# Running nearly all matmuls of an attention and feed-forward kernel as two 64-row array tiles

## Chip, core, metric

The kernel runs on one core of a Trainium2 chip. The metric is the device time of one execution in microseconds (us).

## The reference, cut to what matters

```python
# q: 8 x 16 x 384 x 64, k and v: 8 x 4 x 384 x 64 (each k/v head serves 4 q heads), float32
scores = (1/8) * q @ k.T
attn   = exp(scores - max) / sum
x      = attn @ v                    # then reordered to 3072 tokens x 1024
out    = relu(x @ w_in)**2 @ w_out   # w_in 1024 x 2048, w_out 2048 x 1024
```

There are 8 batches. The kernel works on head pairs, 8 to a batch, so 64 pairs in all. It leaves out the maximum, which the small inputs allow.

## The kernel before

A small recorder takes every operation with the buffers that it reads and writes, and puts in the semaphores. The order in which the program *adds* operations is the order in which each engine is given them. An instruction that waits holds up those behind it.

Scores of one pair are 64-row matmuls (a head has 64 dimensions), one head on the lower and one on the upper half of the array. They fill one stretch of 4.5 PSUM banks, and a single exponential empties it:

```python
def scores_pair(p):
    def piece(pe, x, j, c0, c1):                 # x: head of the pair, so array half
        rows = slice(64 * x, 64 * x + 64)
        return pe.matmul(sc_flat[:, x*half + j*S + c0 : ...], kt[rows, ...], qt[rows, c0:c1])
    first = run([(0, 2, 256, 384)], sc_keys)
    run([(1,1,0,384), (0,0,0,384), (1,2,0,128), (0,1,0,128), (1,2,128,384), (0,1,128,384)], sc_keys)
    run([(1,0,0,384), (0,2,0,256)], sc_keys, after=[first])
    R.add("scalar", lambda e: e.activation(dst, src, AF.Exp, scale=0.125), ...)   # 128 x 2304
```

All else contracts over 128 rows and uses the whole array: attention times V (`attend`, 18 matmuls of 65 columns a pair, into the accumulator bank `po`), the up projection (8 matmuls of 384 columns per output tile, then relu on VectorE and square on ScalarE) and the down projection (16 of 512 columns, then a copy on VectorE).

The main loop puts feed-forward work of the batch before between the pieces of each pair. `PER_PAIR` says how many ns of it. The second batch (`n // NPB == 1`) gets 2600 ns a pair, the later ones 4700 and 5100, because it must save some of the first batch's feed-forward for a pause (`LULL`) before the third batch, while q and k of that batch are transposed:

```python
PER_PAIR = {1: 2600.0, 2: 4700.0, **{b: 5100.0 for b in range(3, B + 1)}}
for n in range(NPB, NP + 1):                     # pair n; the first batch has code of its own
    if n == 2 * NPB:
        ...; prepare(2); prepare_v(2); fill(LULL)
    scores_pair(n)
    fill(per * 0.4);  attend(n - 1, 0)
    fill(per * 0.2);  attend(n - 1, 1);  put_x(n - 1)
    ...
    fill(per * 0.4)
while next(ffn, None): pass                      # the feed-forward of the last batch
```

The softmax here doesn't subtract the row's maximum and nothing guards it: scores larger than these inputs give would overflow.

## Time and profile before

| | before |
|---|---|
| median | 437.3 us |
| PE busy | 99% |
| ScalarE, VectorE busy | 46%, 37% |
| pair in the second batch | 3.87 us |
| pair in later batches | about 6.4 us |

The head of the page: busy us of each engine, share of the span and number of instructions; then the chain that ended last.

```profile
PE 429.8 (99%) x3637; PEld 239.9 (55%) x3637; DVE 160.7 (37%) x345; ACT 198.9 (46%) x210; POOL 48.2 (11%) x62
...
PE 97%; DVE 1%; DMA 1%; issue 0%; ACT 0%
```

TensorE is the limit. The groups of instructions say what it does (line, engine, operation, output and inputs, shapes, count | busy us, mean ns | idle us before them):

```profile
L433 PE MATMUL f_ps<-xT,w_in_sb 128*128 128x384 bf16 x1016 | 181.8, 326 | 1.0 <-DMA xT<-o_sb 1.0
...
L391 ACT ACTIVATE expT<-sc_ps 128x2304 bf16<-128x2304 f32 x56 | 116.8, 2085 | 105.1 <-PE sc_ps L374 103.3
...
L402 PE MATMUL po<-v_aug,expT 128*128 128x65 bf16 x1143 | 56.6, 194 | 0.7 <-DVE o_sb L415 0.4
```

A matmul's recorded 326 ns, whose end is modelled by the profiler, overlaps with the next. What it costs is the distance from one start to the next: 162 ns for 384 columns, 216 for 512, 32 for 65. The second batch's stretch of the chain (start us, us, what) is TensorE alone, with a pair every 3.87 us, although a pair's exponential takes 2.1 us of it:

```profile
43.44 0.60 PE sc_ps L374 x8
44.03 0.76 PE f_ps L433 x4
44.79 0.28 PE po L402 x9
45.07 0.65 PE f_ps L433 x4
45.72 0.28 PE po L402 x9
46.01 1.30 PE f_ps L433 x8
47.31 0.59 PE sc_ps L374 x8
```

The list of PE's waits (engine, what it writes and line <- what it waited for: us in total, times, longest) has none of scores for the exponential. Its only wait for `po`, 0.4 us, falls in the first batch:

```profile
PE f_ps L273 <- DVE warm L221: 1.1, 1, 1.1
PE f_ps L433 <- DMA xT<-o_sb: 1.0, 1, 1.0
PE po L402 <- DVE o_sb L415: 0.4, 1, 0.4
...
```

The scores are where TensorE loses time without waiting for anyone. In the timeline of a later batch (start, us, engine, line, operation, shapes, count):

```profile
202.83 0.65 PE L433 MATMUL f_ps<-xT,w_in_sb 128*128 128x384 bf16 x3
203.42 0.66 PE L374 MATMUL sc_ps<-qT,kT 64*128 64x128 bf16 x9
204.01 1.31 PE L433 MATMUL f_ps<-xT,w_in_sb 128*128 128x384 bf16 x7
```

The third up matmul starts at 203.158 by the trace. Its columns need until 203.32, but the scores start only at 203.416, 96 ns later; their last columns have run at 203.917, and the next whole-array matmul starts at 204.012, 95 ns later.

### The profile page before, as it was taken

The numbers are of one execution on the slowest core, as the hardware profiler recorded it, in microseconds if no ns is written. First come the engines' busy times: TensorE is split into PE (matmuls) and PEld (weight loads), VectorE is DVE, ScalarE is ACT, GpSimd is POOL, SyncE is SP. The second block draws the span as 40 slices with busy tenths as digits, with TensorE's granted clock in tenths as the row PEclk, the third lists the DMA queues.
The fourth block names the chain that finished last, engine by engine and source line by source line (L and its number), as shares of the span: only waits on it lengthen the run. The fifth ranks groups of instructions, "written<-read, shape, count | busy, mean of one in ns | idle before, by whom it ended". The sixth has DMA issues, their size and how long they took to land.

```text
span 435.2 us, 8284 instructions
## 1 busy us (share of the span) xinstructions
PE 429.8 (99%) x3637; PEld 239.9 (55%) x3637; DVE 160.7 (37%) x345; ACT 198.9 (46%) x210; POOL 48.2 (11%) x62
## 2 busy tenths in 40 slices
PE   8999999999999999999999999999999999999997
PEld 4666654565545654566555665456645565546544
DVE  2665423344223433244322442234422344224412
ACT  4866760466333663266423654335742565303400
POOL 5850001031000300022000300003000000000000
PEclk9999999999999999999999999999999999999999
DMA  8999999539721937229622756229462100120012
GB/s 228 196 197 204 188 182 197 149 34 105 175 85 50 118 71 125 85 54 114 128 83 69 98 72 144 69 89 115 47 153 68 59 20 20 58 91 24 2 56 88
DMA packets 96084, 44.71 MB, mean 103 GB/s; under 512 B 74416, under 2 KB 90032, under 8 KB 96048
## 3 DMA queue, kind: packets, MB, share of 16 engines
q0 software_dynamic: 34288, 16.65, 30.3%
q1 hardware_dynamic: 58720, 25.28, 25.0%
q10 hardware_dynamic: 3040, 2.26, 1.7%
q8 instruction: 28, 0.46, 0.5%
q14 instruction: 8, 0.07, 0.0%
HBM read 35.65 MB, written 12.58 MB: 111 GB/s over the span
## 4 chain that ended last, share of the span: by engine, by line
PE 97%; DVE 1%; DMA 1%; issue 0%; ACT 0%
PE f_ps L451 39%; PE f_ps L433 39%; PE po L402 8%; PE sc_ps L374 8%; PE f_ps L273 1%; PE sc_ps L357 1%; PE sc_ps L295 1%; DMA xT<-o_sb 1%; PE f_ps L295 0%; DVE o_sb L415 0%; PE sc_ps L433 0%; DVE qT L303 0%; ACT expT L363 0%; DVE kT L303 0%; DVE k_dup L320 0%
## 5 line engine op out<-in xcount | busy, mean ns | idle before, releaser
L433 PE MATMUL f_ps<-xT,w_in_sb 128*128 128x384 bf16 x1016 | 181.8, 326 | 1.0 <-DMA xT<-o_sb 1.0
L451 PE MATMUL f_ps<-w_out_sb,h2T 128*128 128x512 bf16 (+2 forms) x784 | 180.0, 375 | 0.0
L391 ACT ACTIVATE expT<-sc_ps 128x2304 bf16<-128x2304 f32 x56 | 116.8, 2085 | 105.1 <-PE sc_ps L374 103.3
L433 PEld LDWEIGHTS f_ps<-xT,w_in_sb 128*128 128x128 bf16 x1016 | 92.4, 98 | 61.6 <-issue 6.6
L442 ACT ACTIVATE h2T<-hr 128x384 bf16<-128x384 f32 x128 | 66.6, 521 | 101.1 <-DVE hr L440 99.5
L451 PEld LDWEIGHTS f_ps<-w_out_sb,h2T 128*128 128x128 bf16 x784 | 70.2, 97 | 75.9 <-issue 5.3
L440 DVE TENSOR_SCALAR hr<-f_ps 128x384 f32<-128x384 f32 x127 | 70.6, 557 | 105.8 <-PE f_ps L433 105.7
L459 DVE COPY y_sb<-f_ps 128x512 f32<-128x512 f32 (+2 forms) x49 | 33.4, 681 | 111.9 <-PE f_ps L451 111.4
L402 PEld LDWEIGHTS po<-v_aug,expT 128*128 128x128 bf16 x1143 | 51.8, 98 | 22.6 <-ACT expT L363 2.0
L402 PE MATMUL po<-v_aug,expT 128*128 128x65 bf16 x1143 | 56.6, 194 | 0.7 <-DVE o_sb L415 0.4
L374 PE MATMUL sc_ps<-qT,kT 64*128 64x128 bf16 (+2 forms) x504 | 37.2, 271 | 0.0
L415 DVE TENSOR_TENSOR o_sb<-po,rinv 128x384 bf16<-128x384 f32 x64 | 35.5, 554 | 2.2
L374 PEld LDWEIGHTS sc_ps<-qT,kT 64*128 64x128 bf16 x504 | 20.6, 94 | 21.4 <-issue 15.0
L412 DVE RECIPROCAL rinv<-po 128x6 f32<-128x6 f32 x64 | 12.2, 191 | 39.6 <-PE po L402 39.6
L167 POOL DMA_DIRECT2D k_st<-in_k_dram x7 | 5.4, 775 | 166.7 <-DMA xT<-o_sb 166.7
L363 ACT ACTIVATE expT<-sc_ps 128x768 bf16<-128x768 f32 x24 | 18.5, 810 | 3.1 <-PE sc_ps L357 2.5
L320 POOL COPY k_dup<-k_st 128x1536 bf16<-128x1536 bf16 x6 | 8.8, 1469 | 42.9 <-DMA k_st<-in_k_dram 42.9
L341 POOL COPY v_aug<-v_st 128x768 bf16<-128x768 bf16 x6 | 5.0, 832 | 43.0 <-DMA v_st<-in_v_dram 43.0
L357 PE MATMUL sc_ps<-qT,kT 64*128 64x384 bf16 x48 | 8.3, 341 | 0.2
L181 POOL DMA_DIRECT2D q_st<-in_q_dram x7 | 8.2, 1178 | 0.0
L273 PE MATMUL f_ps<-warm 128*128 128x256 bf16 x29 | 7.2, 371 | 1.1 <-DVE warm L221 1.1
L189 POOL DMA_DIRECT2D w_in_sb<-in_moe_w_in_dram x8 | 7.0, 887 | 0.0
(46 smaller groups left out, 57.6 us busy)
## 6 DMA issues: line engine op xcount, KB each, us to landing
out_dram<-y_sb SPq DMA_DIRECT2D x47, 256.0 KB, 2.0
q_st<-in_q_dram POOLq DMA_DIRECT2D x7, 768.0 KB, 11.1
w_in_sb<-in_moe_w_in_dram POOLq DMA_DIRECT2D x8, 512.0 KB, 11.4
w_out_sb<-in_moe_w_out_dram POOLq DMA_DIRECT2D x2, 2048.0 KB, 34.0
k_st<-in_k_dram POOLq DMA_DIRECT2D x7, 192.0 KB, 3.6
v_st<-in_v_dram POOLq DMA_DIRECT2D x7, 192.0 KB, 10.6
xT<-o_sb SPq DMA_TRANSPOSE x56, 2.4
q_f<-in_q_dram ACTq DMA_DIRECT2D x1, 768.0 KB, 9.3
```

The lines of the kernel that those rows point to most:

```text
L357: m = pe.matmul(sc_ps[:, 2 * u + x, 0:S], kt[rows, j * 128:(j + 1) * 128], qt[rows, :])
L363: R.add("scalar", lambda e: e.activation(dst, src, AF.Exp, scale=0.125), reads=[("sc", 2 * u), ("sc", 2 * u + 1)], writes=[("expT", p % NE ...
L374: return pe.matmul(sc_flat[:, at + c0:at + c1], kt[rows, j * 128:(j + 1) * 128], qt[rows, c0:c1])
L391: R.add("scalar", lambda e: e.activation(dst, src, AF.Exp, scale=0.125), reads=sc_keys, writes=[("expT", p % NEX, j) for j in range(NJ)])
L402: m = pe.matmul(acc[:, i, s, :], expT[p % NEX][:, j, f * 128:(f + 1) * 128], v_aug[b % 2][:, g * NJ + j, :], start=(j == 0), stop=(j == NJ ...
L412: R.add("vector", lambda e: e.reciprocal(rinv_v, acc[:, :, ss, D:D + 1]), reads=[acc_key], writes=[("rinv", p % 2)])
L415: R.add("vector", lambda e: e.tensor_tensor(o_sb[p % NO][:, :, ss, :], acc[:, :, ss, 0:D], rb, ALU.mult), reads=[acc_key, ("rinv", p % 2)] ...
L433: m = pe.matmul(acc[:, 0:S], w_in_sb[:, kc, c * 128:(c + 1) * 128], xT[b % NXT][:, kc, :], start=(kc == 0), stop=(kc == NKC - 1))
L440: R.add("vector", lambda e: e.tensor_scalar_max(hr[r][:, :], acc[:, 0:S], 0.0), reads=[key], writes=[("hr", r)])
L442: R.add("scalar", lambda e: e.activation(h2T[b % 2][:, c, :], hr[r][:, :], AF.Square), reads=[("hr", r)], writes=[("h2T", b % 2, c)])
L451: m = pe.matmul(f_ps[u][:, 0:c1 - c0], h2T[b % 2][:, c, i * 128:(i + 1) * 128], w_out_sb[:, c, jj * 512 + c0:jj * 512 + c1], start=(c == 0 ...
L459: R.add("vector", lambda e: e.tensor_copy(y_sb[yb][:, c0:c1], f_ps[u][:, 0:c1 - c0]), reads=[("f_ps", u)], writes=[("y", yb, c0)])
```

## The change

From the second batch up to the last feed-forward *every* matmul uses 64 rows. A contraction over 128 rows becomes a lower half on tile 0 and, later, an upper half on tile 64 that adds to the same accumulator. The Trainium skill, "TensorEngine Tiling (Array Packing)", section "Gotcha 1: PSUM Pressure", says that different row tiles cannot access one PSUM bank simultaneously and that software must see to it. The upper half of a job therefore follows when the lower half has finished, and meanwhile the lower tile works on the next job in another bank. The intent: the array never changes its mode, and the scores simply join the stream.

Scores and exponential come in two halves of three banks each, the same three banks, because feed-forward now takes four banks in turn. The program plans the two tiles with a small clock of its own. Two side effects: the third batch's pairs get 4500 instead of 4700 ns, and its transposes are issued 2600 ns of feed-forward later in the pause. The diff, cut:

```diff
+    GAP = 450.0                                  # upper half: not before 450 ns after the lower
+    def push(lo, hi, done=None, prev=None):      # emit the lower half now, queue the upper half
+        for ns, fn in lo:
+            catch_up(clock["lo"])                # first emit upper pieces that are due by now
+            last = fn(after)
+            clock["lo"] += ns
+        behind.append(dict(hi=list(hi), ready=clock["lo"] + GAP, after=[last], done=done, ...))
+    F_BANKS = [sc_ps bank 3, sc_ps bank 4, f_ps0, f_ps1]
+    def row_scores(p, half):
+        both([piece(i) for i in range(3)])       # three 64 x 384 matmuls into sc_ps banks 0, 1, 2
+        R.add("scalar", lambda e: e.activation(expT[...3 * half:3 * half + 3...], sc_ps[:, 0:3, 0:S], AF.Exp, ...))
+    def row_attend(p, then=None): ...            # 18 lower, later 18 upper; then VectorE frees po
+    def row_up(b, c, r): ...                     # 8 lower, later 8 upper; then relu and square
+    def row_down(b, jj): ...                     # three banks, in chunks of 6, 5, 5 matmuls
...
-    PER_PAIR = {1: 2600.0, 2: 4700.0, ...}
+    PER_PAIR = {1: 2600.0, 2: 4500.0, ...}
+    by_rows[0] = True
     for n in range(NPB, NP + 1):
+        ahead = (per - 600.0) / 2
-            scores_pair(n)
-        fill(per * 0.4)
-            attend(n - 1, 0)
-        ...
+            row_scores(n, 0)
+        fill(ahead)
+            row_attend(n - 1, ...)
+            row_scores(n, 1)
+        fill(per - ahead)
+    by_rows[0] = False                           # the last feed-forward: whole array again
```

More of the change, by code (lines that the diff above doesn't have):

```diff
@@ L146, in bass_gqa_attention__then__ffn_squared_relu_kernel @@
     qT = [sb(f"qT{i}", [128, NPB, S]) for i in range(2)]
-    expT = [sb(f"expT{i}", [128, NJ, 2 * S]) for i in range(NEX)]
+    expT = [sb(f"expT{i}", [128, 2 * NJ, S]) for i in range(NEX)]
     rinv = [sb(f"rinv{i}", [128, NJ, 2], f32) for i in range(2)]
@@ L360, in scores_unit @@
         R.add("tensor", sc, reads=keys, writes=[("sc", 2 * u), ("sc", 2 * u + 1)])
-        src = sc_ps[:, 2 * u:2 * u + 2, 0:S].rearrange("p x (t c) -> p x t c", t=NJ)
-        dst = expT[p % NEX][:, j, :].rearrange("p (t x c) -> p x t c", x=2, t=NJ)
+        src = sc_ps[:, 2 * u:2 * u + 2, 0:S]
+        dst = expT[p % NEX][:, 2 * j:2 * j + 2, :]
         R.add("scalar", lambda e: e.activation(dst, src, AF.Exp, scale=0.125),
-              reads=[("sc", 2 * u), ("sc", 2 * u + 1)], writes=[("expT", p % NEX, j)])
-    def scores_pair(p):
-        kt, qt, keys, k_keys = operands(p)
-        keys = keys + k_keys
-        half = NJ * S
-        def piece(pe, x, j, c0, c1):
-            at = x * half + j * S
-            rows = slice(64 * x, 64 * x + 64)
-            return pe.matmul(sc_flat[:, at + c0:at + c1], kt[rows, j * 128:(j + 1) * 128], qt[rows, c0:c1])
-        def run(pieces, writes, after=()):
-            def mm(pe):
-                for pc in pieces:
-                    m = piece(pe, *pc)
-                return m
-            return R.add("tensor", mm, reads=keys, writes=writes, after=after)
-        sc_keys = [("sc", i) for i in range(5)]
-        first = run([(0, 2, 256, 384)], sc_keys)
-        run([(1, 1, 0, 384), (0, 0, 0, 384), (1, 2, 0, 128), (0, 1, 0, 128), (1, 2, 128, 384),
-             (0, 1, 128, 384)], sc_keys)
-        run([(1, 0, 0, 384), (0, 2, 0, 256)], sc_keys, after=[first])
-        src = sc_flat[:, 0:2 * half].rearrange("p (x a c) -> p x a c", x=2, c=128)
-        dst = expT[p % NEX].ap().rearrange("p j (t x c) -> p x (j t) c", x=2, t=NJ)
-        R.add("scalar", lambda e: e.activation(dst, src, AF.Exp, scale=0.125),
-              reads=sc_keys, writes=[("expT", p % NEX, j) for j in range(NJ)])
+              reads=[("sc", 2 * u), ("sc", 2 * u + 1)], writes=[("expT", p % NEX, 2 * j), ("expT", p % NEX, 2 * j + 1)])
     def attend(p, s, alone=False):
@@ L401, in av @@
                 for j in range(NJ):
-                    m = pe.matmul(acc[:, i, s, :], expT[p % NEX][:, j, f * 128:(f + 1) * 128],
+                    m = pe.matmul(acc[:, i, s, :], expT[p % NEX][:, 2 * j + f % 2, f // 2 * 128:f // 2 * 128 + 128],
                                   v_aug[b % 2][:, g * NJ + j, :], start=(j == 0), stop=(j == NJ - 1))
             return m
-        R.add("tensor", av, reads=[("expT", p % NEX, j) for j in range(NJ)] +
+        R.add("tensor", av, reads=[("expT", p % NEX, u) for u in range(2 * NJ)] +
               [("v_aug", b % 2), ("v_one", b % 2)], writes=[acc_key])
@@ L423, in put_x, with catch_up @@
             reads=[("o_sb", p % NO, x) for x in range(2)], writes=[("xT", b % NXT, c)], dma=f"xt{p % 8}")
+    GAP = 450.0
+    clock = {"lo": 0.0, "hi": 0.0}
+    behind = []
+    def catch_up(until):
+        while behind:
+            job = behind[0]
+            begin = max(clock["hi"], job["ready"])
+            if begin > until:
+                return
+            ns, fn = job["hi"].pop(0)
+            job["last"] = fn(job["after"])
+            job["after"] = ()
+            clock["hi"] = begin + ns
+            if not job["hi"]:
+                behind.pop(0)
+                job["over"] = True
+                if job["done"]:
+                    job["done"]()
@@ new lines, in push @@
+    def push(lo, hi, done=None, prev=None):
+        while prev is not None and not prev["over"]:
+            clock["lo"] += 100.0
+            catch_up(clock["lo"])
+        after = [prev["last"]] if prev is not None else ()
+        total = 0.0
+        for ns, fn in lo:
+            catch_up(clock["lo"])
+            last = fn(after)
+            after = ()
+            clock["lo"] += ns
+            total += ns
+        job = dict(hi=list(hi), ready=clock["lo"] + GAP, after=[last], done=done, over=False)
+        behind.append(job)
+        return job, total
@@ new lines, in both, with drain, next_bank @@
+    def both(pieces):
+        catch_up(clock["lo"])
+        clock["hi"] = max(clock["hi"], clock["lo"])
+        for x, ns, fn in pieces:
+            fn(())
+            clock["lo" if x == 0 else "hi"] += ns
+    def drain():
+        catch_up(float("inf"))
+    ROWS = (slice(0, 64), slice(64, 128))
+    F_BANKS = [(sc_ps[:, 3], ("sc", 3)), (sc_ps[:, 4], ("sc", 4)), (f_ps[0].ap(), ("f_ps", 0)), (f_ps[1].ap(), ("f_ps", 1))]
+    owner = [None] * 4
+    turn = [0]
+    def next_bank():
+        i = turn[0] % 4
+        turn[0] += 1
+        while owner[i] is not None and not owner[i]["over"]:
+            clock["lo"] += 100.0
+            catch_up(clock["lo"])
+        return i
@@ new lines, in row_scores, with piece @@
+    def row_scores(p, half):
+        kt, qt, keys, k_keys = operands(p)
+        def piece(i):
+            u = 3 * half + i
+            j, x = u // 2, u % 2
+            rows = ROWS[x]
+            return x, 162.0, lambda after: R.add(
+                "tensor", lambda pe: pe.matmul(sc_ps[:, i, 0:S], kt[rows, j * 128:(j + 1) * 128], qt[rows, :]),
+                reads=keys + k_keys[j:j + 1], writes=[("sc", i)], after=after)
+        both([piece(i) for i in range(3)])
+        R.add("scalar", lambda e: e.activation(expT[p % NEX][:, 3 * half:3 * half + 3, :], sc_ps[:, 0:3, 0:S],
+                                               AF.Exp, scale=0.125),
+              reads=[("sc", i) for i in range(3)], writes=[("expT", p % NEX, 3 * half + i) for i in range(3)])
@@ new lines, in row_attend, with piece, done @@
+    def row_attend(p, then=None):
+        b, g = p // NPB, (p % NPB) // 2
+        def piece(r, f, j):
+            rows = ROWS[r]
+            return 33.0, lambda after: R.add(
+                "tensor", lambda pe: pe.matmul(
+                    po_v[:, f % NJ, f // NJ, :], expT[p % NEX][rows, 2 * j + f % 2, f // 2 * 128:f // 2 * 128 + 128],
+                    v_aug[b % 2][rows, g * NJ + j, :], start=(r == 0 and f == 0 and j == 0), stop=(r == 1),
+                    skip_group_check=True),
+                reads=[("expT", p % NEX, 2 * j + f % 2), ("v_aug", b % 2), ("v_one", b % 2)], writes=["po"], after=after)
+        def done():
+            rinv_v = rinv[p % 2].ap().unsqueeze(3)
+            R.add("vector", lambda e: e.reciprocal(rinv_v, po_v[:, :, :, D:D + 1]),
+                  reads=["po"], writes=[("rinv", p % 2)])
+            R.add("vector", lambda e: e.tensor_tensor(o_sb[p % NO][:, :, :, :], po_v[:, :, :, 0:D],
+                                                      rinv_v.to_broadcast([128, NJ, 2, D]), ALU.mult),
+                  reads=["po", ("rinv", p % 2)], writes=[("o_sb", p % NO, x) for x in range(2)])
+            landed = put_x(p)
+            if then:
+                then(landed)
+        lo, hi = ([piece(r, f, j) for f in range(2 * NJ) for j in range(NJ)] for r in range(2))
+        push(lo, hi, done)
@@ new lines, in row_up, with piece, done @@
+    def row_up(b, c, r):
+        i = next_bank()
+        acc, key = F_BANKS[i]
+        def piece(h, kc):
+            rows = ROWS[h]
+            return 162.5, lambda after: R.add(
+                "tensor", lambda pe: pe.matmul(acc[:, 0:S], w_in_sb[rows, kc, c * 128:(c + 1) * 128],
+                                               xT[b % NXT][rows, kc, :], start=(h == 0 and kc == 0),
+                                               stop=(h == 1 and kc == NKC - 1), skip_group_check=True),
+                reads=[("w_in", c * 128 // WC), ("xT", b % NXT, kc)], writes=[key], after=after)
+        def done():
+            R.add("vector", lambda e: e.tensor_scalar_max(hr[r][:, :], acc[:, 0:S], 0.0),
+                  reads=[key], writes=[("hr", r)])
+            R.add("scalar", lambda e: e.activation(h2T[b % 2][:, c, :], hr[r][:, :], AF.Square),
+                  reads=[("hr", r)], writes=[("h2T", b % 2, c)])
+        lo, hi = ([piece(h, kc) for kc in range(NKC)] for h in range(2))
+        owner[i], total = push(lo, hi, done)
+        return total
@@ new lines, in row_down, with piece, done @@
+    def row_down(b, jj):
+        banks, jobs = [None] * NJ, [None] * NJ
+        chunks = ((0, 6), (6, 11), (11, 16))
+        for c0, c1 in chunks:
+            for i in range(NJ):
+                if c0 == 0:
+                    banks[i] = next_bank()
+                acc, key = F_BANKS[banks[i]]
+                def piece(h, c, i=i, acc=acc, key=key):
+                    rows = ROWS[h]
+                    return 216.0, lambda after: R.add(
+                        "tensor", lambda pe: pe.matmul(acc, h2T[b % 2][rows, c, i * 128:(i + 1) * 128],
+                                                       w_out_sb[rows, c, jj * 512:(jj + 1) * 512],
+                                                       start=(h == 0 and c == 0), stop=(h == 1 and c == NFC - 1),
+                                                       skip_group_check=True),
+                        reads=[("w_out", jj), ("h2T", b % 2, c)], writes=[key], after=after)
+                def done(i=i, acc=acc, key=key):
+                    yb = (b * 2 * NJ + jj * NJ + i) % NY
+                    R.add("vector", lambda e: e.tensor_copy(y_sb[yb][:, :], acc), reads=[key], writes=[("y", yb, 0)])
+                    rows = out[b * S:(b + 1) * S, :].rearrange("(p j) f -> j p f", j=NJ)[i]
+                    R.add("sync", lambda e: e.dma_start(rows[:, jj * 512:(jj + 1) * 512], y_sb[yb][:, :]),
+                          reads=[("y", yb, 0)], writes=[("out", b, i, jj, 0)], dma=f"y{yb}_0")
+                lo, hi = ([piece(h, c) for c in range(c0, c1)] for h in range(2))
+                jobs[i], total = push(lo, hi, done if c1 == NFC else None, jobs[i])
+                owner[banks[i]] = jobs[i]
+                yield total
@@ L426, in bass_gqa_attention__then__ffn_squared_relu_kernel @@
     tiles = [0]
+    by_rows = [False]
     def up_step(b, c, k0, k1, u, r):
+        drain()
         acc, key = (f_ps[u].ap(), ("f_ps", u)) if u < 2 else (sc_ps[:, 2], ("sc", 2))
@@ L446, in down_step @@
     def down_step(b, i, jj, part, u, c0=0, c1=512):
+        drain()
         yb = (b * 2 * NJ + jj * NJ + i) % NY
@@ L472, in feed_forward @@
         for c in range(first, NFC):
-            for k in range(0, NKC, 4):
-                yield up_step(b, c, k, k + 4, tiles[0] % 2, tiles[0] % NHR)
+            if by_rows[0]:
+                yield row_up(b, c, tiles[0] % NHR)
+            else:
+                for k in range(0, NKC, 4):
+                    yield up_step(b, c, k, k + 4, tiles[0] % 2, tiles[0] % NHR)
             tiles[0] += 1
         for jj in range(2):
+            if by_rows[0]:
+                yield from row_down(b, jj)
+                continue
             for i in range(NJ):
@@ L495, in bass_gqa_attention__then__ffn_squared_relu_kernel @@
     LULL = 11000.0
-    PER_PAIR = {1: 2600.0, 2: 4700.0, **{b: 5100.0 for b in range(3, B + 1)}}
+    PER_PAIR = {1: 2600.0, 2: 4500.0, **{b: 5100.0 for b in range(3, B + 1)}}
     def fill(ns):
@@ L556, in bass_gqa_attention__then__ffn_squared_relu_kernel, with load_next @@
         fill(600.0)
+    by_rows[0] = True
     for n in range(NPB, NP + 1):
-        per = PER_PAIR[n // NPB]
+        b, c = n // NPB, n % NPB
+        per = PER_PAIR[b]
+        ahead = (per - 600.0) / 2
+        def load_next(landed):
+            for load in (load_k, load_q, load_v):
+                load(b + 1, [landed])
         if n == 2 * NPB:
-            fill(per * 0.5)
-            attend(n - 1, 0)
-            attend(n - 1, 1)
-            put_x(n - 1)
+            fill(ahead)
+            row_attend(n - 1)
+            fill(2600.0)
             prepare(2)
             prepare_v(2)
-            fill(LULL)
+            fill(LULL - 2600.0)
             ready[0] = 1
         if n < NP:
-            scores_pair(n)
-        fill(per * 0.4)
+            row_scores(n, 0)
+        fill(ahead)
         if n > NPB and n != 2 * NPB:
-            attend(n - 1, 0)
-        fill(per * 0.2)
-        if n > NPB and n != 2 * NPB:
-            attend(n - 1, 1)
-            landed = put_x(n - 1)
-            if n % NPB == 1 and 2 * NPB < n < (B - 1) * NPB:
-                for load in (load_k, load_q, load_v):
-                    load(n // NPB + 1, [landed])
-        if 2 * NPB < n < (B - 1) * NPB:
-            if n % NPB == 4:
-                prepare(n // NPB + 1)
-            if n % NPB == 7:
-                prepare_v(n // NPB + 1)
-        fill(per * 0.4)
-        ready[0] = max(0, n // NPB - 1)
+            row_attend(n - 1, load_next if c == 1 and 2 <= b < B - 1 else None)
+        if n < NP:
+            row_scores(n, 1)
+        if 2 * NPB < n < (B - 1) * NPB:
+            if c == 4:
+                prepare(b + 1)
+            if c == 7:
+                prepare_v(b + 1)
+        fill(per - ahead)
+        ready[0] = max(0, b - 1)
+    by_rows[0] = False
     while next(ffn, None):
```

## The prediction

> **What bounds it now.** TensorE, without a pause. The page shows PE busy 99% at a granted clock of 1.0; the chain of waits gives PE 97% of the span; PE's own waits sum to under 3 us. From start to start in the trace, an up-projection matmul (128x384) costs 162 ns, a down-projection matmul (128x512) 216 ns: their columns at full rate. So the 171 us of up and 168 us of down can't shrink; there is gain only where TensorE doesn't stream.
>
> **Where it loses time.** The scores of a head pair (9 matmuls on 64-row tiles, 2304 columns) stand among 128-row matmuls, in 56 pairs after the first batch. The last 128-row matmul before them takes 258 instead of 162 ns to the next start (or 312 instead of 216); the scores then take 596 ns, of which the last 256 columns take 202 where 109 suffice inside the group; the next 128-row matmul takes 173. Together some 705 ns a pair. The Trainium skill, "TensorEngine Tiling (Array Packing)", Key Properties, says that changing the tiling mode drains TensorE; this trace agrees, with 95 ns on each side. In between, the row tiles run truly side by side: each one's starts are 56, 109 and 163 ns apart for 128, 256 and 384 columns.
>
> **What the change does.**
> - Removes both mode changes of each pair, and the unequal ends. Six 64x384 matmuls, three a tile, need 3 x 162.5 = 488 ns: 217 ns x 56 = 12.2 us saved, all on the critical path.
> - Doubles the matmuls and weight loads, but two run at a time, so up and down keep 162 and 216 ns per two halves, if the rate seen in the scores lasts and holds when accumulating.
> - Attention times V: 18 matmuls of 65 columns a pair cost 32.3 ns each; planned as 33 a tile: +0.7 us. One tile's short matmuls now stand in program order with the other's long ones and wait for their turn: an estimate of 20 ns a pair, +1 us; five times that if the two tiles' weight loads share one path, which no trace shows.
> - The upper tile starts one job (1.3 us) plus 0.45 us late, and the lower idles as long at the end: half the array for 1.75 us twice, +1.75 us.
> - Splits the exponential: 128x768 takes 810 and 128x2304 2085 ns, so about 1130 each, +170 ns of ScalarE a pair, off the path. Four accumulator banks in turn, each held about 3.8 us (two jobs, gap, a 557 ns eviction) of a 5.2 us turn: no wait.
> - First batch and last feed-forward (41.6 us) unchanged.
>
> **Predicted time.** 437.3 - 12.2 + 0.7 + 1.0 + 1.75 = 428.5 us, range 422 to 438. Chances: faster by over 2% 0.47, within 2% 0.43, slower 0.10.
>
> **What would show each step.** (a) Each row tile's starts 162 and 216 ns apart in up and down jobs, over many microseconds; PE still near 99%. (b) The scores without the 95 ns pauses. (c) During attention times V, the other tile's long matmuls still 162 or 216 ns apart; more would be the shared path. (d) PE's waits on VectorE or its own signals under 3 us in sum. (e) The exponential at about 1130 ns, PE not waiting for it.
>
> **What would make it wrong.** Long row-tiled streams below full rate (1% of 360 us is 3.6 us); the program order of two unequal streams costing tens of ns at each step; waits of the upper half for the lower's last write, if 450 ns is too little; banks free late. These push towards slower. Better than 422 would need attention times V below 32 ns a matmul.

## The result

| | before | after |
|---|---|---|
| median | 437.3 us | 436.47 us |
| ratio, 95% interval | | 0.9982 [0.9965, 0.9999] |
| span of the profiled run | 435.2 us | 434.3 us |
| pair in the second batch | 3.87 us | 4.87 us |
| second batch, first scores to those of the third batch | 43.86 us | 50.36 us |

A ratio here is the mean time of one kernel's fast runs over that of the other's of the same rounds, so it is not quite the ratio of the medians. The time fell inside the range, but of 8.8 us forecast, 0.8 came: a gain that was forecast nearly cancels against a loss that was not.

The head of the page after, and the same groups:

```profile
PE 422.9 (97%) x5995; PEld 315.6 (73%) x5997; DVE 163.6 (38%) x345; ACT 206.8 (48%) x266; POOL 48.4 (11%) x62
...
PE 91%; DVE 3%; ACT 3%; DMA 1%; issue 0%
...
L471 ACT ACTIVATE expT<-sc_ps 128x1152 bf16<-128x1152 f32 x112 | 126.0, 1125 | 112.0 <-PE sc_ps L467 68.9
...
L481 PE MATMUL po<-v_aug,expT 64*128 64x65 bf16 x2016 | 81.4, 190 | 1.8 <-DVE o_sb L491 1.8
...
L467 PE MATMUL sc_ps<-qT,kT 64*128 64x384 bf16 x336 | 54.9, 323 | 3.5 <-ACT expT L471 3.4
```

The exponential takes 1125 ns, close to the predicted 1130, but in two places TensorE now stands idle: the scores for the exponential, attention for VectorE. ACT and DVE now take 3% of the chain each, where they took 0% and 1%. The waits of PE (us in total, times, longest):

```profile
PE sc_ps L467 <- ACT expT L471: 3.4, 7, 0.6
PE po L481 <- DVE o_sb L491: 1.8, 6, 0.7
```

Where the row tiles should gain, they do. The same place in a later batch, where the scores now start in step with the stream:

```profile
204.95 0.32 PE L508 MATMUL f_ps<-xT,w_in_sb 64*128 64x384 bf16 x1
204.98 0.32 PE L508 MATMUL sc_ps<-xT,w_in_sb 64*128 64x384 bf16 x1
205.11 0.48 PE L467 MATMUL sc_ps<-qT,kT 64*128 64x384 bf16 x3
205.31 0.32 PE L508 MATMUL sc_ps<-xT,w_in_sb 64*128 64x384 bf16 x1
205.44 0.32 PE L508 MATMUL f_ps<-xT,w_in_sb 64*128 64x384 bf16 x1
```

From 204.95 to 205.11 to the lower tile's next up matmul at 205.44 there are no pauses: each tile starts a matmul every 162 ns, the scores among them.

Where it loses is the second batch. One turn of its chain:

```profile
47.85 1.03 ACT expT L471
48.87 0.05 issue
48.92 0.36 PE sc_ps L467 x3
...
50.18 0.20 DVE rinv L489
50.38 0.02 issue
50.40 0.57 DVE o_sb L491
50.97 0.05 issue
51.01 0.20 PE po L481
...
51.61 0.56 DVE hr L514
52.17 0.02 issue
52.19 0.52 ACT h2T L516
52.72 1.03 ACT expT L471
```

Read it as a circle of 4.87 us. The exponential frees the three banks, and the next scores go in. Behind them in TensorE's order stands the upper half of the attention begun before. When that is done VectorE takes 0.2 + 0.57 us to free `po`, for which the next pair's lower half waits, and with it everything behind. A feed-forward tile thereby finishes late; its relu is late, its square is late, and the next exponential stands behind that square in ScalarE's order. (Its scores have been in the banks since about 52.0 us; it starts at 52.6, right behind the square.) Only the exponential's end lets the next scores in.

A balance of the whole span makes this countable. The trace does not record an array tile, so I put each matmul on its tile by the order of the program (all but two of 5997 are in the trace). I then subtracted from each distance between two starts on a tile the time of the columns (0.417 ns each plus 2.5 ns, fitted to the observed 56, 162 and 216 ns for 128, 384 and 512 columns). What is left is idle time of that tile; a whole-array matmul counts on both:

| idle us (lower tile / upper tile) | before | after |
|---|---|---|
| second batch | 1.8 / 2.0 | 8.4 / 10.3 |
| third batch up to the last feed-forward | 12.9 / 13.0 | 5.8 / 4.1 |

The mean of the tiles changes by +7.4 us in the second batch and by -8.0 us afterwards: -0.6 us in sum, against -0.9 us between the profiled spans. Counting gaps of over 150 ns alone, 4.8 us of the second batch's idle time on the lower and 6.6 us on the upper tile lie in front of scores (2.1 of the 6.6 are the upper tile's late start), and 3.1 us on the lower tile in front of attention.

### The profile page after: what moved, and what is told of

Its sections match the earlier page's. It is cut to its first block, busy times and chain, and to the rows that moved or that the text cites. A ratio compares the mean times of both kernels' runs of the same rounds, so it can differ in the third digit from the quotient of the medians.

```text
span 434.3 us, 12988 instructions
## 1 busy us (share of the span) xinstructions
PE 422.9 (97%) x5995; PEld 315.6 (73%) x5997; DVE 163.6 (38%) x345; ACT 206.8 (48%) x266; POOL 48.4 (11%) x62
## 4 chain that ended last, share of the span: by engine, by line
PE 91%; DVE 3%; ACT 3%; DMA 1%; issue 0%
PE f_ps L535 15%; PE sc_ps L535 15%; PE f_ps L508 14%; PE sc_ps L508 13%; PE po L481 11%; PE sc_ps L467 6%; PE f_ps L563 6%; PE f_ps L582 5%; ACT expT L471 2%; DMA xT<-o_sb 1%; PE f_ps L273 1%; PE sc_ps L357 1%; PE po L374 1%; DVE o_sb L491 1%; PE sc_ps L295 1%; DVE hr L514 1%
## 5 line engine op out<-in xcount | busy, mean ns | idle before, releaser
L471 ACT ACTIVATE expT<-sc_ps 128x1152 bf16<-128x1152 f32 x112 | 126.0, 1125 | 112.0 <-PE sc_ps L467 68.9
L535 PE MATMUL f_ps<-w_out_sb,h2T 64*128 64x512 bf16 x704 | 140.0, 376 | 0.0
L535 PE MATMUL sc_ps<-w_out_sb,h2T 64*128 64x512 bf16 x640 | 131.7, 376 | 0.0
L508 PE MATMUL sc_ps<-xT,w_in_sb 64*128 64x384 bf16 x864 | 128.7, 322 | 0.0
L508 PE MATMUL f_ps<-xT,w_in_sb 64*128 64x384 bf16 x832 | 121.1, 323 | 0.9 <-DMA xT<-o_sb 0.9
L481 PEld LDWEIGHTS po<-v_aug,expT 64*128 64x128 bf16 x2016 | 77.0, 94 | 15.3 <-DVE o_sb L491 4.4
L481 PE MATMUL po<-v_aug,expT 64*128 64x65 bf16 x2016 | 81.4, 190 | 1.8 <-DVE o_sb L491 1.8
L508 PEld LDWEIGHTS sc_ps<-xT,w_in_sb 64*128 64x128 bf16 x864 | 70.9, 94 | 11.3
L508 PEld LDWEIGHTS f_ps<-xT,w_in_sb 64*128 64x128 bf16 x832 | 68.8, 94 | 14.2 <-DMA xT<-o_sb 1.9
L563 PE MATMUL f_ps<-xT,w_in_sb 128*128 128x384 bf16 x168 | 29.1, 326 | 0.8 <-DVE y_sb L543 0.8
```

Source lines behind the costliest of these rows:

```text
L471: R.add("scalar", lambda e: e.activation(expT[p % NEX][:, 3 * half:3 * half + 3, :], sc_ps[:, 0:3, 0:S], AF.Exp, scale=0.125), reads=[("sc ...
L481: "tensor", lambda pe: pe.matmul(po_v[:, f % NJ, f // NJ, :], expT[p % NEX][rows, 2 * j + f % 2, f // 2 * 128:f // 2 * 128 + 128], v_aug[b ...
L508: "tensor", lambda pe: pe.matmul(acc[:, 0:S], w_in_sb[rows, kc, c * 128:(c + 1) * 128], xT[b % NXT][rows, kc, :], start=(h == 0 and kc == ...
L535: "tensor", lambda pe: pe.matmul(acc, h2T[b % 2][rows, c, i * 128:(i + 1) * 128], w_out_sb[rows, c, jj * 512:(jj + 1) * 512], start=(h == ...
L563: m = pe.matmul(acc[:, 0:S], w_in_sb[:, kc, c * 128:(c + 1) * 128], xT[b % NXT][:, kc, :], start=(kc == 0), stop=(kc == NKC - 1))
```

## The experiments

The theory: the row tiles give what they should from the third batch on, and the second batch loses nearly as much, because its pairs are too short for the round through ScalarE and VectorE. The rival: twice the matmuls, nearly all of which now signal (4800 instead of 705), give the gain back a little everywhere. Within the theory two causes compete: the exponential in two halves on the same three banks, and the upper half, which comes late and holds `po`.

### Row tiles from the third batch on

```diff
+    # pairs 8 to 15: loop body, scores_pair and attend of the kernel before, in the new layout of expT
-    by_rows[0] = True                  # before the loop
     if n == 2 * NPB:
+        attend(n - 1, 0); attend(n - 1, 1); put_x(n - 1)
+        by_rows[0] = True
```

> Second batch as in the kernel before (whole-array matmuls, one exponential a pair), row tiles only from the third batch on. My theory: the row tiles save about 8 us from the third batch on (idle time of a tile there 12.9 us before, 5.0 us after), and the second batch gives 6.3 us back, because its pairs are short and TensorE waits there for ScalarE and VectorE. Then this run takes about 430 us (437.3 - 7.9 + 0.95 for the late start of the upper tile). Rival: the row tiles give their gain back a little everywhere (twice the matmuls, nearly every one signalling); then about 437 us.

Measured: 431.57 us, ratio 0.9864 [0.9848, 0.9881]. The two waits for the exponential and for `po` shrink to one of 0.6 us and one of 0.3 us, the latter in the first batch. The rival's 437 is out. The missing 1.2 us is partly a longer wait for transposed attention output (xT): 1.6 us, where the longest before was 1.0. It does not lie at the seam, where the row tiles begin at about 70 us, but at 185.7 us:

```profile
PE f_ps L536 <- DMA xT<-o_sb: 1.6, 1, 1.6
```

### Row tiles in the second batch only

```diff
             fill(LULL - 2600.0)
             ready[0] = 1
+            by_rows[0] = False         # from here on the loop body of the kernel before
```

> The reverse: row tiles only in the second batch, whole-array matmuls and one exponential a pair from the third on. My theory: only the loss is left, about 444 us (437.3 + 6.3 + about 1 for the drain), with pairs of about 4.9 us in the second batch against 3.9 before. Rival (loss spread evenly): about 437 us, pairs in the second batch near 3.9 us.

Measured: 447.07 us, ratio 1.0219 [1.0204, 1.0234]. The second batch's waits are those of the changed kernel to the tenth (3.4 us in 7 waits for the exponential, 1.8 us in 6 for `po`). It came out 3 us slower than expected. In the balance its second batch loses what the changed kernel's does (8.4 and 10.3 us idle on the two tiles), which is 7.4 us more than before and not the 6.3 that were entered. The seam after it costs another 2.6 us in the mean of the tiles, where about 1 was entered: the last upper half runs alone (nine matmuls, 1.96 us of the chain), and the first scores and the first up matmuls each wait for VectorE to copy a bank:

```profile
PE f_ps L591 <- DVE y_sb L571: 0.8, 1, 0.8
PE sc_ps L374 <- DVE y_sb L571: 0.5, 1, 0.5
```

So the loss belongs to the second batch. The two parts alone, +9.8 and -5.7 us against their runs of the kernel before, add up to +4.1 and not to the whole's -0.8: by the balance some 3.5 us of the difference are the seam that each has and the whole has not; the rest was not traced.

### The exponential cut in half

```diff
+        w = S // 2 if p // NPB == 1 else S
-        e.activation(expT[p % NEX][:, 3 * half:3 * half + 3, :], sc_ps[:, 0:3, 0:S], AF.Exp, scale=0.125)
+        e.activation(expT[p % NEX][:, 3 * half:3 * half + 3, 0:w], sc_ps[:, 0:3, 0:w], AF.Exp, scale=0.125)
```

Its output is wrong, which doesn't matter for the time. The comparison nevertheless let it pass, probably because the scores are small and the old values in the buffer close to the right ones.

> Wrong result on purpose: the changed kernel, but in the second batch the exponential covers only the first 192 of 384 columns of each bank, about 0.65 us instead of 1.13. If the scores' wait for the exponential sets the pace there (it is on the chain once a pair with 1.03 us), a pair shortens by about 0.45 us and the whole by about 3.5 us, to 433. If the pace is set by the late upper half (the attention accumulator freed late, feed-forward evictions late), the time stays at 436.

Measured: 433.33 us, ratio 0.9904 [0.9887, 0.992]. A pair takes 4.39 us instead of 4.87. The waits of PE for the exponential are gone from the list, those for VectorE are untouched:

```profile
PE po L482 <- DVE o_sb L492: 1.9, 6, 0.7
PE f_ps L273 <- DVE warm L221: 1.1, 1, 1.1
```

So the exponential's length helps to set the pace, and it is not alone: with that wait gone a pair still takes 0.5 us more than before. (A shorter instruction in the circle would help whatever made the circle long; this run does not tell the split of the exponential from its place behind the square.)

### Shorter jobs, so that the upper half follows sooner

```diff
-        lo, hi = ([piece(h, kc) for kc in range(NKC)] for h in range(2))
-        owner[i], total = push(lo, hi, done)
+        for k0, k1 in ((0, 4), (4, 8)) if b == 0 else ((0, 8),):
+            lo, hi = ([piece(h, kc) for kc in range(k0, k1)] for h in range(2))
+            job, t = push(lo, hi, done if k1 == NKC else None, job)
```

> The changed kernel, but the up projection of the first batch's feed-forward (which fills the second batch's pairs) is handed to the tiles in jobs of 4 matmuls instead of 8, so the upper half lags by 0.65 + 0.45 us instead of 1.3 + 0.45. If the late upper half is on the chain once a pair, a pair shortens by up to 0.65 us while up projections fill it (about 7 of the 8 pairs): 432 us. If only the exponential counts: 436.

Measured: 443.22 us, ratio 1.0128: a failed experiment, which tells nothing about the lag. Both jobs of a tile accumulate in one bank, so the program makes the lower half's second job wait until the upper half has done its first. The balance shows 12.2 us of new idle time on the lower tile in front of up matmuls, and the chain shows it as groups of four matmuls that wait for one another:

```profile
58.75 0.66 PE f_ps L508 x4
59.41 0.05 issue
```

It fits that the down projection of the changed kernel, which also cuts its contraction into chunks, goes through three banks in turn.

### Whole array, but scores and exponential in two halves

```diff
-    by_rows[0] = True
-            row_attend(n - 1, ...)
+            attend(n - 1, 0); attend(n - 1, 1); landed = put_x(n - 1)
```

> Everything on the whole array again, but scores and exponential in two halves a pair as in the changed kernel: four array-mode changes a pair instead of two. If a change costs 95 ns, a half takes 325 + 190 + 10 ns, two halves 1050 ns against 705: +19 us over 56 pairs, about 456 us in all. On the second batch the theories part: if the two exponentials on the same three banks are what TensorE waits for there, its pairs grow to 4.9 us here too, and the waits of scores for the exponential are near 7 us; if it also takes the late upper half, the pairs there grow only by the mode changes, to about 4.2 us.

Measured: 460.12 us, ratio 1.0524 [1.0507, 1.0542]. From the third batch on the price is as expected: of the 23.1 us, 6.5 fall in the second batch (50.41 us, against 43.86) and 0.2 before it, leaving 16.4 us, or 341 ns a pair, where 345 was expected. That is the cost of two more mode changes and uneven ends, measured by adding them. In the second batch a pair takes 4.78 us, near the 4.9 of the first alternative and without any late upper half, but the waits of scores for the exponential come to 3.2 us and not to the 7 that were expected with it. Here is one such pair; the scores at 48.20 wait although the array is free:

```profile
47.00 0.73 PE L374 MATMUL po<-v_aug,expT 128*128 128x65 bf16 x18
48.20 0.49 PE L467 MATMUL sc_ps<-qT,kT 64*128 64x384 bf16 x3 [0.48 <-ACT expT L471]
48.63 2.12 PE L563 MATMUL f_ps<-xT,w_in_sb 128*128 128x384 bf16 x12
```

And the chain that leads there:

```profile
46.02 0.57 DVE hr L570
...
46.60 0.52 ACT h2T L572
47.13 1.03 ACT expT L471
48.15 0.05 issue
48.20 0.49 PE sc_ps L467 x3
```

About 0.35 us of the longer pair are the additional mode changes, the remaining 0.56 us are this wait; the other half's scores do not wait. So scores and exponential in two halves on the same banks, in this order of instructions, are enough to stall the second batch.

The order is part of it. The scores that this exponential reads were done by about 46.4 us, but ScalarE had a feed-forward tile's square before it, which itself waited for the relu (hr), and so it started some 0.6 us later: as much as the wait. The changed kernel shows the same, and there ScalarE idles 7.0 us in six gaps in front of such squares. No run put the exponential before the square, so how much of the stall such an order would remove stays open.

The waits for `po` are absent here, so they seem to take the late upper half (in the turn shown above, upper-half attention stands in the chain before `po` is freed). That is read from the comparison of two runs; no run freed `po` alone.

### Longer pairs in the second batch

```diff
-    PER_PAIR = {1: 2600.0, 2: 4500.0, ...}
+    PER_PAIR = {1: 3400.0, 2: 4500.0, ...}
+        if n == 2 * NPB - 1:               # one pair earlier than in the changed kernel
+            prepare(2); prepare_v(2)
```

> The changed kernel with 3400 instead of 2600 ns of feed-forward between the scores in each pair of the second batch, and the third batch's transposes of q and k issued one pair earlier so that they are still in time. My theory (the pairs are too short for the round through ScalarE and VectorE): with 0.8 us more the waits nearly vanish; pairs of about 4.5 us without waits, a tile's idle time in the second batch falls from about 9 us to under 4; but less work is left for the pause before the third batch, where up to 3 us may come back: about 432 us. Rival (the waits come from the row tiles' order of instructions, whatever the length of a pair): waits as before, pairs of 4.9 us or more, 436 us or worse.

Measured: 433.61 us, ratio 0.9921 [0.9903, 0.9938]. The wait for `po` is down to one of 0.2 us, that for the exponential nearly halved:

```profile
PE sc_ps L467 <- ACT expT L471: 1.9, 4, 0.7
PE f_ps L508 <- DMA xT<-o_sb: 1.5, 2, 0.9
```

In the stretch from 36 to 90 us the tiles idle 4.3 and 6.0 us. That is more than the hoped 4: feed-forward is handed out in whole jobs of 1.3 us, so pairs vary from 3.9 to 5.8 us, and the short ones still wait. The row tiles are as before and only the pairs are longer, so the rival that their order of instructions stalls whatever the length of a pair is out too.

### A version that beats both kernels

```diff
     # on top of row tiles from the third batch on
-                    yield up_step(b, c, k, k + 4, tiles[0] % 2, ...)
+                    yield up_step(b, c, k, k + 4, 2 if (b, c) == (B - 1, 0) else tiles[0] % 2, ...)
```

> A version meant to beat both: row tiles from the third batch on (431.6 us in the earlier run), and the first whole-array tile after them writes a PSUM bank that has long been free, instead of one that VectorE is still emptying (a wait of 0.8 us at the end of the row tiles in every run so far). Expected 0.8 us less: about 430.8 us, ratio to the kernel before 0.985.

Measured: 430.9 us, ratio 0.9856 [0.9834, 0.9879]. The wait of 0.8 us for VectorE's copy is gone from the list. Whether the second edit adds anything to the first can't be said from the times: the intervals overlap.

## Why the prediction was wrong

- **What bounds the kernel, and what the mode changes cost: right.** 95 ns at each side were read before, and adding two changes a pair cost 341 ns a pair in later batches, where 345 was computed.
- **The gain of the row tiles: right in mechanism and nearly in size.** 217 ns a pair over 48 pairs are 10.4 us. The balance from the third batch on shows 8.0 us less idle time, after about 1.9 us lost at the end, where the two tiles change back to the whole array (2.8 us on the lower, 0.95 on the upper tile). Without that end it is 9.9 us, or 205 ns a pair.
- **Long row-tiled streams at full rate: right.** From 90 to 385 us the median distance is 162 ns on each tile for 384 columns and 216 for 512, and 99% of them lie within 3 ns of it.
- **Attention and program order: too dark.** Attention took 31.6 ns a matmul in the mean, as before, not 33, and the other tile kept its 162 and 216 ns. I had assumed that a tile's matmul waits its turn in the program's order; the trace shows otherwise (below).
- **Start and end: right in kind, too small.** 2.1 us on the upper tile at the start (in 0.7 of which the lower one, too, waits for the exponential), 2.8 on the lower and 0.95 on the upper at the end: 2.9 us in the mean of the tiles, where 1.75 was entered. 0.8 us of the end is a wait for VectorE's copy of a bank.
- **The exponential "about 1130 each, +170 ns of ScalarE a pair, off the path": this is the step that failed.** The size is right (1125 ns), the place wrong. The prediction gives no reason for "off the path", and the only period that it names is a turn of 5.2 us, that of later batches. In the second batch a pair has 2.6 us of feed-forward and passed in 3.87 us. There the *same* three banks must be filled, read and filled again twice a pair, each exponential in its order on ScalarE, and TensorE waited in 7 places, 3.4 us in all, where "PE not waiting for it" was forecast. A pair grew to 4.87 us. Halving the exponential there took 3.1 us off.
- **"Four accumulator banks ... no wait": true for these four, but a fifth was forgotten.** `po` is single, and PE waited for it 1.8 us in 6 waits, all in the second batch; that the late upper half holds it longer is argued above, not tested alone.
- So I had the sum of the gain and none of the loss: the second batch cost 7.4 us of idle time that appears in no term of mine.

## What to carry to other kernels

Before calling added work on another engine off the path, look at the *shortest* period in which it recurs, not at its share of the span. Be wary of splitting an eviction whose halves share the banks of one whole: that doubles the number of round trips per unit of work. (Halves with banks of their own were not tried here: feed-forward and `po` took five of the eight banks that the program uses.) And where a change pays in some stages only, switch it by stage: the same row tiles gave 1.4% once the short pairs were left out.

## What the Trainium skill lacked or had wrong

- "TensorE: Matmul & The Clock Gate", Part 3, says that matmuls are strict FIFO in start and end, with no reordering. In the changed kernel, starts are in order only *within* a row tile. At 41.947 us an up matmul of the upper tile starts before three attention matmuls of the lower tile that stand before it in the program and start at 41.971, 42.004 and 42.033. (Ends are modelled in this trace, so it says nothing of them.)
- "TensorEngine Tiling (Array Packing)", Key Properties, says that changing the mode drains TensorE, but not at what price. Here it is 95 ns of lost streaming at each change between 128-row and 64-row matmuls.
- The same page gives no sustained rate. Two row tiles, accumulating in two banks, each held the whole-array pace (162 ns for 384, 216 ns for 512 columns) over nearly 300 us, with twice the weight loads; attention's 31.6 ns a matmul did not suffer from the other tile's loads.
- Its section "PSUM Bottleneck" warns that evacuation does not get faster with tiling. The page does not say that an engine far from full can still set the pace. In this program feed-forward on row tiles took four banks, the scores kept three and went through them in two halves, and a pair of the second batch took 4.87 instead of 3.87 us, with ScalarE at 48% of the span.
